# Attention outputs kept as features by tokens, their softmax sums turned by DMA, and GpSimd and SyncE in program order

## The chip, the cores and the metric

One core of a Trainium2 chip runs the whole program. Its engines are TensorE (PE; PEld is its weight load), VectorE (DVE), ScalarE (ACT), GpSimd (POOL) and SyncE (SP, which only issues transfers). The metric is the device time of one execution in microseconds.

## The reference

A block with adaptive layer norm, softmax attention and a gated feed-forward part, all in float32:

```python
# x: 2048 tokens x 576; 32 heads of 18; the feed-forward width is 4608
x = A_x
mod = (silu(c) @ w_mod)                          # sa, ca, ga, sb, cb, gb: 576 each
h = layernorm(x) * (1 + ca) + sa
q, k, v = (h @ wqkv) split into 32 heads of 18
p = softmax(q @ k.T * 18 ** -0.5)
o = p @ v                                        # heads side by side: 2048 x 576
x = x + ga * (o @ wo)
h = layernorm(x) * (1 + cb) + sb
x = x + gb * ((sigmoid(h @ w_gate) * (h @ w_up)) @ w_down)
```

## The kernel before

There are three stages. The first normalizes the tokens and projects q, k and v. The second is attention, with much other work laid into it. The third ("gated" stage) computes the feed-forward part, with two levels of sums and differences of blocks that save products.

**Attention.** The loop over `u` has 32 units: a half of the tokens (1024 queries) times a pair of heads. Inside, `kt` runs over 16 tiles of 128 keys. Work is written out for pairs of steps by the strings in `STEPS`: `t` is a score product of a head and a chunk of 512 queries, followed by its exponential on ACT; `m` is one of the 64 products per unit whose row maxima DVE takes for a coming unit (`maxima`, driven by `turn`, 24 products ahead); `V`, or `A` and `B` in halves, is the product of exponentials and values (`values`) for all four head-chunks at once. The values have a column of ones, so that the 19th of each 32 result rows is the softmax sum. The result of a unit is a bank of 128 partitions (4 groups of 32: head, chunk) by 512 queries: features by tokens.

When a unit is done, `taken` copies the bank to `oT` on ACT (L673). `outputs`, in the pair at `kt` 2 of the next unit, turns it with four transposes on PE (L683), copies it back to `oT` on ACT (L699), takes reciprocals on DVE (L702) and multiplies on GpSimd (L705) into a table of tokens by features: `Oa` for the first half, a tile `big` for the second, together the list `Os`. For `kt` 2 and 4 there are orders of their own in `STEPS`.

Other work goes along one piece per pair, at the letter `G`. `down_parts` (units 4 to 14, on GpSimd) splits and scales `w_down`; `first_rows` (step 240 to 439) projects tiles 0 to 7 of the first half's rows with `wo` and prepares the operands of the gated stage; `last_rows_project` (from step 440) projects tiles 8 to 15, from 384 of the 576 features. Both use `project_o`, which transposes each tile of the table back to features by tokens on PE (L772, L789), copies it by DVE (L778) and splits it into a high and a low part on GpSimd (L779, L780). Where a coming piece has products, the pair is "heavy" and takes the order `full`, with whole value products; else the pair is "halved". A heavy pair at `kt` 2 or 12 is put off (`hold`).

`spread` turns the maxima of a unit into two rows of its queries (four small transfers, L590). `load_heads(u + 2)` loads queries and keys of the unit after the next by eight transfers on SyncE, at the start of unit `u`. The queries' and keys' buffers are those of unit `u - 1`.

The remaining 192 features of the second half are stored (`oend`) and projected in `last_rows`, a generator that runs between the products of the gated stage and transposes them again (L1526, L1534).

**What sets the order.** Engines named in `manual_schedule` keep the order in which the program emits their instructions. The others get an order from the framework's planner, by its own costs. In attention PE and ACT were named; SyncE, DVE and GpSimd were planned. From the eighth product of the gated stage on, PE, DVE and ACT are named. Every engine executes its queue in order, so an instruction that waits holds those behind it. `paced` makes an instruction wait for the last exponential emitted so far.

Of the kernel before, what the change touches and what calls it, by code (L numbers as in the profile page):

```python
# [23 lines left out]
P = 128  # L24
S = 2048
# [62 lines left out]
def tile_block(ctx, tc, x_in, wqkv, wo, w_gate, w_up, w_down, c_in, w_mod, out):  # L88
# [206 lines left out]
    oend = dram.tile([P, 8, D - DL], F32, name="oend")  # L295
# [338 lines left out]
    Os = [Oa]  # L634
# [33 lines left out]
    def taken():  # L668

        if "whole" in state:  # L670
            half, p, acc = state.pop("whole")
            oT = epool.tile([P, 512], F32, name="oT")
            nc.scalar.copy(oT, acc)  # L673
            state["end"] = (half, p, oT)

    def outputs():

        if "end" not in state:
            return
        half, p, oT = state.pop("end")  # L680
        tp = bank().rearrange("p (b q) -> p b q", q=P)
        for b in range(4):
            nc.tensor.transpose(tp[:, b, :], oT[:, b * P : (b + 1) * P], ident)  # L683

        yield
        tq = tp.rearrange("p b (j e) -> p j b e", e=32)
        rec = epool.tile([P, 4, 4], F32, name="rec")
        if half == 1 and p == H // 2 - 1:
            nc.vector.reciprocal(rec, tq[:, :, :, DH])
            state["last"] = epool.tile([P, 512], F32, name="oT")[:, 0 : 16 * DH].rearrange("p (t e) -> p t e", t=8)  # L690
            for h in range(2):
                nc.vector.tensor_tensor(
                    state["last"][:, :, h * DH : (h + 1) * DH].rearrange("p (c b) e -> p c b e", c=2),
                    tq[:, 2 * h : 2 * h + 2, :, 0:DH],
                    rec[:, 2 * h : 2 * h + 2, :].unsqueeze(3).to_broadcast([P, 2, 4, DH]),
                    op=ALU.mult,
                )
            return
        nc.scalar.copy(oT, tp.rearrange("p b q -> p (b q)"))  # L699
        yield  # L700
        tq = oT.rearrange("p (b j e) -> p j b e", j=4, e=32)
        nc.vector.reciprocal(rec, tq[:, :, :, DH])  # L702
        for h in range(2):
            f0 = (2 * p + h) * DH
            nc.gpsimd.tensor_tensor(  # L705
                Os[half][:, :, f0 : f0 + DH].rearrange("p (c b) e -> p c b e", c=2),
                tq[:, 2 * h : 2 * h + 2, :, 0:DH],
                rec[:, 2 * h : 2 * h + 2, :].unsqueeze(3).to_broadcast([P, 2, 4, DH]),
                op=ALU.mult,
            )  # L710


# [4 lines left out]
    def load_wo():  # L717
# [31 lines left out]
        for _ in range(4):  # L749
            yield  # L750
# [3 lines left out]
    def project_o(t):  # L754

        wo_h, wo_l, we = weights
        if t <= 8:
            held_rows[:] = temp([P, 2048], F32R), temp([P, 2048], F32)
        T, T_ = held_rows
        if t < 8:  # L760
            xt, full, od = T_[:, 0:D], T_[:, 1024:1536], T_[:, 1536:1664]
        else:
            T, T_ = T[:, 1024 * (t % 2) : 1024 * (t % 2) + 1024], T_[:, 960 * (t % 2) : 960 * (t % 2) + 960]
            xt, full = T_[:, 0:D], T_[:, D : D + 384]
        nc.gpsimd.dma_start(xt, x_rows[:, t, :])
        src = Os[t // 8][:, t % 8, :]
        n = 4 if t < 8 else DL // P
        oh = T[:, 0 : n * P]
        ol = T[:, 512 : 512 + n * P]
        pt = bank()  # L770
        for i in range(n):
            nc.tensor.transpose(pt[:, i * P : (i + 1) * P], src[:, i * P : (i + 1) * P], ident)  # L772
        if t >= 12:
            nc.vector.tensor_copy(oh, pt[:, 0 : n * P])
            nc.vector.tensor_sub(ol, pt[:, 0 : n * P], oh.bitcast(F32))  # L775
        else:
            full = full[:, 0 : n * P]
            nc.vector.tensor_copy(full, pt[:, 0 : n * P])  # L778
            nc.gpsimd.tensor_copy(oh, full)  # L779
            nc.gpsimd.tensor_sub(ol, full, oh.bitcast(F32))  # L780
        yield None if t < 8 else "g"
        if t < 8:
            om = T[:, 1024:1152]
            omh = T[:, 1152:1280]
            nc.gpsimd.tensor_copy(
                od.rearrange("p (a e) -> p a e", e=64), src[:, DM:D].unsqueeze(1).to_broadcast([P, 2, 64])
            )
            pt = bank()
            nc.tensor.transpose(pt[:, 0:P], od, ident)  # L789
            nc.vector.tensor_copy(od, pt[:, 0:P])  # L790
            nc.gpsimd.tensor_copy(om[0:64], od[0:64])
            nc.gpsimd.tensor_copy(omh[64:P], od[64:P])
            nc.gpsimd.tensor_sub(om[64:P], od[64:P], omh[64:P].bitcast(F32))
            yield "g"
        for h in range(2):
            cols = slice(h * HALF, (h + 1) * HALF)
            ts_ = []
            for i in range(n):
                a, b = oh[:, i * P : (i + 1) * P], ol[:, i * P : (i + 1) * P]
                ts_ += [(a, wo_h[:, i, cols]), (a, wo_l[:, i, cols]), (b, wo_h[:, i, cols])]  # L800
            if t < 8:
                ts_ += [(om, we[:, 0, cols]), (om, we[:, 1, cols])]
            acc = bank()
            for i, (a, w) in enumerate(ts_):
                nc.tensor.matmul(acc[:, :HALF], a, w, start=i == 0, stop=i == len(ts_) - 1)  # L805
            to = Oa[:, t, :] if t < 8 else xt
            nc.vector.tensor_add(to[:, cols], xt[:, cols], acc[:, 0:HALF])
            yield None if h else "g"
        if t >= 8:
            nc.gpsimd.dma_start(x1p[:, t - 8, :], xt)  # L810
# [64 lines left out]
    def first_rows():  # L875
        yield from load_wo()
        for t in range(8):
            yield from project_o(t)
# [118 lines left out]
    def last_rows_project():  # L997
        for t in range(8, NT):
            yield from project_o(t)

# [36 lines left out]
    rows1 = last_rows_project()  # L1037
    downs = down_parts()
    for u in range(UNITS):
        half, p = divmod(u, H // 2)  # L1040
        qs, ks = heads(u)
        if 0 < u < UNITS - 2:
            load_heads(u + 2)
        if u == H // 2:
            Os.append(big.tile([P, 8, 640], F32, name="big"))
        for kt in range(NT):
# [3 lines left out]
            if kt % 2 == 0:  # L1050
                heavy = state.get("next") == "g"
                hold = heavy and (kt == 2 or kt == 12 and u < UNITS - 1)
                halved = step >= 10 and (hold or not heavy)
                rows = FROM0 <= step < FROM1
                order = two_steps(STEPS["full" if not halved else "rows" if rows else kt if kt in STEPS else "half"])
            probs = [None] * 4
            for does, h, c in order[kt % 2]:
# [4 lines left out]
                elif does in "OSG":  # L1062
                    if halved and kt == 2:
                        follow.append(outputs())
                        next(follow[-1], None)
# [23 lines left out]
            pending.append((half, p, kt, probs))  # L1089
            if u in (1, 3):  # L1090
# [29 lines left out]
            if u == UNITS - 1 and kt == 3:  # L1120
                nc.sync.dma_start(oend[:, :, 0 : D - DL - 2 * DH], Os[1][:, :, DL : D - 2 * DH])
# [12 lines left out]
    for _ in outputs():  # L1134
        pass
    manual.close()
    nc.sync.dma_start(oend[:, :, D - DL - 2 * DH :], state["last"])
# [373 lines left out]
    def last_rows():  # L1511

        def psum():
            return pd.tile([P, 512], F32, name="d")

        with tc.tile_pool(name="fin", bufs=1, side="right") as pool:
            w = pool.tile([P, 2, 2, D], F32R, name="w")
            nc.gpsimd.dma_start(w, wod)
            for t0 in (0, 4):
                od = pool.tile([P, 4, 256], F32, name="od")  # L1520
                nc.sync.dma_start(od[:, :, 0:192], oend[:, t0 : t0 + 4, :])
                nc.sync.dma_start(od[:, :, 192:256], oend[:, t0 : t0 + 4, 128:192])
                yield 1.4, 5 if t0 == 0 else 2
                pt = psum()
                for j in range(4):
                    nc.tensor.transpose(pt[:, j * P : (j + 1) * P], od[:, j, 0:P], ident)  # L1526
                oh = pool.tile([P, 512], F32R, name="oh")
                ol = pool.tile([P, 512], F32R, name="ol")
                nc.vector.tensor_copy(oh, pt)
                nc.vector.tensor_sub(ol, pt, oh.bitcast(F32))  # L1530
                yield 1.4, 1
                pt = psum()
                for j in range(4):
                    nc.tensor.transpose(pt[:, j * P : (j + 1) * P], od[:, j, P:256], ident)  # L1534
                om = pool.tile([P, 512], F32R, name="om")
                omh = pool.tile([P, 512], F32R, name="omh")
                nc.vector.tensor_copy(om[0:64], pt[0:64])
                nc.vector.tensor_copy(omh[64:P], pt[64:P])
                yield 0.7, 0
# [278 lines left out]
```

## Time and profile before

| | |
|---|---|
| median of 3 runs | 2801.53 us (2798.26 to 2804.0) |
| profiled execution: time, span | 2804.88 us, 2803.1 us |
| granted TensorE clock, mean | 0.998 |
| busy PE, DVE, ACT, POOL | 2771.9, 2306.3, 1609.3, 814.6 us |
| attention | first exponential at 236.1 us, last value products until 1532.9 us |

The profiled execution took 2804.88 us, of which the span, first to last instruction, is 2803.1. In the profile's rows a time in front is a start in microseconds from the span's begin, then the duration, the engine, the line of the kernel, the operation and `out<-in` by the program's names, with the number of instructions merged in the row. In rows of groups, busy time and the mean duration in nanoseconds follow the bar, then the idle time of the engine ahead of them and what ended it. Buffers from `bank` are called `s`, those of the rows' temporaries `t`.

### The profile page before, as it was taken

What the parts mean: (1) busy time and instruction counts of PE and PEld (TensorE: products, weight loads), DVE (VectorE), ACT (ScalarE), POOL (GpSimd) and SP (SyncE); (2) the same over time, 40 slices, a digit from 0 to 9 for tenths busy, and PEclk for the clock granted to TensorE, in tenths of its full rate; (3) what the DMA queues carried; (4) which work ended last, traced back from release to release, by engine and by line L of the source; (5) the groups of instructions that cost most, each with busy time, mean ns of one, the idle gap of its engine ahead of it and who ended that gap; (6) DMA issues with size and microseconds to landing.
All of it is one profiled execution on the core that took longest, in us unless ns stands there. A gap on an engine that the chain in (4) does not pass through costs nothing.

```text
span 2803.1 us, 50644 instructions
## 1 busy us (share of the span) xinstructions
PE 2771.9 (99%) x18637; PEld 1847.4 (66%) x18637; DVE 2306.3 (82%) x4370; ACT 1609.3 (57%) x3051; POOL 814.6 (29%) x1077
## 2 busy tenths in 40 slices
PE   7999999999999999999999999999999999999999
PEld 5975444444444444444444888888888888888888
DVE  7278999999998888999883778888898677777777
ACT  3215999999999878999888332333333222222221
POOL 3125207888843111663103222232221100000000
PEclk9999999999999999999999999999999999999999
DMA  5344224444432120232127766667767956566653
GB/s 172 121 157 140 78 61 162 171 169 166 172 133 82 36 58 24 98 106 71 43 68 227 273 222 223 240 213 273 278 245 280 339 195 201 194 200 195 200 195 120
DMA packets 170777, 462.59 MB, mean 165 GB/s; under 512 B 21212, under 2 KB 88032, under 8 KB 160416
## 3 DMA queue, kind: packets, MB, share of 16 engines
q1 hardware_dynamic: 150064, 360.72, 38.4%
q0 software_dynamic: 20464, 98.62, 9.9%
q8 instruction: 147, 2.41, 0.4%
q14 instruction: 102, 0.84, 0.1%
HBM read 281.92 MB, written 176.82 MB: 164 GB/s over the span
## 4 chain that ended last, share of the span: by engine, by line
PE 92%; DVE 4%; DMA 2%; issue 2%; POOL 0%; ACT 0%; SPq 0%; DVEq 0%; ACTq 0%; POOLq 0%
PE x L1225 26%; PE o L656 19%; PE s L1084 12%; PE s L550 11%; PE d L1375 8%; PE d L1307 6%; PE s L336 4%; PE s L805 2%; PE s L389 1%; DMA out_dram<-Oa 1%; DVE mx L556 1%; PE s L683 1%; DMA wq_raw<-in_A_wqkv_dram 1%; DVE w L1215 0%; DVE Oa L1379 0%
## 5 line engine op out<-in xcount | busy, mean ns | idle before, releaser
L1088 ACT ACTIVATE p<-s 128x512 f32<-128x512 f32 x2048 | 1069.1, 616 | 89.2 <-PE s L1084 62.6
L556 DVE TENSOR_REDUCE mx<-s 128x1 f32<-128x512 f32 x1568 | 1000.9, 683 | 101.3 <-PE s L550 75.1
L656 PE MATMUL o<-p,vaug 128*32 128x256 f32 (+1 forms) x5848 | 595.1, 478 | 0.1
L550 PE MATMUL s<-k,q 54*128 54x512 f32 x1920 | 548.6, 434 | 2.0 <-DVE t L775 1.0
L1084 PE MATMUL s<-q,k 56*128 56x512 f32 x1920 | 527.7, 440 | 0.0
L550 PEld LDWEIGHTS s<-k,q 54*128 54x128 f32 x1920 | 273.4, 184 | 231.9 <-DVE mx L561 88.0
L1084 PEld LDWEIGHTS s<-q,k 56*128 56x128 f32 x1920 | 249.8, 184 | 232.1 <-ACT p L1088 72.9
L1225 PE MATMUL x<-k,w 128*128 128x512 f32 x1512 | 370.0, 392 | 0.0
L1225 PEld LDWEIGHTS x<-k,w 128*128 128x128 f32 x1512 | 276.8, 188 | 53.3 <-PE o L656 0.8
L1375 PE MATMUL d<-wd,hh 128*128 128x288 f32 x1248 | 249.9, 295 | 2.4 <-DVE Oa L1379 2.4
L656 PEld LDWEIGHTS o<-p,vaug 128*32 128x32 f32 x5848 | 116.2, 108 | 203.1 <-issue 187.5
L1225 PE MATMUL x<-big,w 128*128 128x512 f32 x1008 | 245.5, 392 | 0.7 <-DVE u L1724 0.7
L1225 PE MATMUL x<-w,w 128*128 128x512 f32 x1008 | 245.3, 391 | 0.0
L1225 PEld LDWEIGHTS x<-big,w 128*128 128x128 f32 x1008 | 185.1, 188 | 37.0 <-DVE u L1724 1.1
L1225 PEld LDWEIGHTS x<-w,w 128*128 128x128 f32 x1008 | 184.3, 188 | 34.5
L1375 PEld LDWEIGHTS d<-wd,hh 128*128 128x128 f32 x1248 | 202.2, 188 | 6.2 <-DVE Oa L1379 3.1
L1375 PE MATMUL d<-wd,hl 128*128 128x288 f32 x624 | 184.3, 295 | 0.0
L1379 DVE TENSOR_TENSOR Oa<-Oa,d 128x288 f32<-128x288 f32 x312 | 136.6, 453 | 55.1 <-PE d L1375 51.2
L561 DVE CUSTOM_DVE_ANT_0 over<-s,over 128x512 f32<-128x512 f32 x240 | 163.9, 683 | 1.3 <-PE s L1084 1.2
L559 ACT ACTIVATE over<-s 128x512 f32<-128x512 f32 x240 | 145.8, 608 | 11.3 <-PE s L550 9.3
L1234 ACT ACTIVATE sg<-x 128x512 f32<-128x512 f32 x36 | 21.6, 599 | 210.2 <-PE x L1225 210.2
L1206 ACT CAST w<-S 128x768 fp32r<-128x768 f32 x71 | 59.4, 836 | 137.8 <-POOL S L1179 136.0
(275 smaller groups left out, 3898.5 us busy)
## 6 DMA issues: line engine op xcount, KB each, us to landing
ws<-w SPq DMA_DIRECT2D x126, 640.0 KB
w<-ws SPq DMA_DIRECT2D x126, 640.0 KB
wd<-wds SPq DMA_DIRECT2D x19, 1152.0 KB
k<-kd SPq DMA_DIRECT2D x60, 360.0 KB
wds<-w POOLq DMA_DIRECT2D x18, 1152.0 KB, 5.2
wtd<-t POOLq DMA_DIRECT2D x32, 576.0 KB, 5.0
wt<-wtd SPq DMA_DIRECT2D x64, 288.0 KB
wd<-wds SPq DMA_DIRECT2D x52, 288.0 KB
```

Source lines behind the costliest of these rows:

```text
L336: nc.tensor.matmul(acc, w, hT[:, t, cols], start=n == 0, stop=n == len(ts_) - 1)
L550: nc.tensor.matmul(sp, qs[rows, qt * P : (qt + 1) * P], ks[rows, at * 512 : (at + 1) * 512], start=True, stop=True,)
L556: nc.vector.tensor_reduce(to, sp, axis=AX.X, op=ALU.max)
L559: nc.scalar.activation(over, sp, AF.Relu)
L561: nc.vector.tensor_tensor_reduce(out=over, in0=sp, in1=over, scale=1.0, scalar=LOWEST, op0=ALU.add, op1=ALU.max, accum_out=mx[:, h * n + q ...
L656: nc.tensor.matmul(acc[32 * j : 32 * j + 32, cols], vaug[:, kt, (2 * p + h) * VW : (2 * p + h) * VW + 32], probs[2 * c + h][:, cols], star ...
L1084: nc.tensor.matmul(sT, ks[rows, kcols], qs[rows, c * 512 : (c + 1) * 512], start=True, stop=True)
L1088: state["exp"] = nc.scalar.activation(pr, sT, AF.Exp, scale=SCALE)
L1225: nc.tensor.matmul(acc[v], w[:, v, a, :], X[s][:, b, :], start=first and n == 0, stop=n == 6, skip_group_check=not first,)
L1307: nc.tensor.matmul(acc, a[:, rows], w[:, k, :], start=n == 0, stop=n == 2)
L1375: nc.tensor.matmul(acc[:, :HALF], a[:, f, rows], w[:, f, cols], start=n == 0, stop=n == 5)
L1379: nc.vector.tensor_add(Oa[:, t, cols], Oa[:, t, cols], acc[:, :HALF])
```

## The change

The outputs stay features by tokens, so nothing is transposed on PE on their account.

- `taken` copies the bank to `oT`, then stores the four rows of sums (4 x 512) to memory and loads them as 128 x 16 (`sT`). The new `outputs`, a generator advanced at the letter `c`, takes their reciprocals on DVE at `kt` 2 (paced), stores them, loads them repeated over 32 partitions each (`R`, 128 x 512), multiplies `oT` by `R` on GpSimd at `kt` 6 (paced), and at `kt` 14 stores the four blocks of 18 features to `ot` in memory.
- `load_rows` loads rows of `ot` (features by tokens) into `big`, 128 features at a time, at units 14 and 16 for the first half, 26 and 27 for the second.
- `project_rows` replaces `project_o`: `rows_parts` splits a tile's columns of `big` on GpSimd alone, one tile ahead; the products and additions are as they were. Two segments per tile remain of four or three; a pause of ten instead of four pieces follows `load_wo`.
- The orders for `kt` 2 and 4 go, and with them the holding of heavy pairs at `kt` 2.
- `load_heads(u + 2)` moves from the start of the unit to behind `kt` 4.
- SyncE and GpSimd are named in attention's `manual_schedule`.
- The last unit's sums and outputs go through `lastd`; `last_rows` loads the sums, takes reciprocals and multiplies on DVE, without transposes.

```diff
-    2: "V m1t0 t1t0 m0m1 O A c m1r0 t1m0 t1t0 G B c x0t1 m1t0",
-    4: "V r0m1 t1t0 m1m0 G A c t0t1 m1t0 B t1m0 m1t0 t1x0",
...
     def taken():
...
+        sT = epool.tile([P, 16], F32, name="sT")
+        to = osums[half * H // 2 + p, 0]
+        nc.sync.dma_start(to, oT[DH::32, :])
+        nc.sync.dma_start(sT, to.rearrange("j (q r) -> (j q) r", r=16))
+        follow.append(outputs(half, p, oT, sT))
+
+    def outputs(half, p, oT, sT):
+
+        while state["kt"] < 2:
+            yield
+        rec = epool.tile([P, 16], F32, name="rec")
+        paced(nc.vector.reciprocal(rec, sT))
+        to = osums[half * H // 2 + p, 1]
+        nc.sync.dma_start(to.rearrange("j (q r) -> (j q) r", r=16), rec)
+        R = state["room"] if "room" in state else bgp.tile([P, 512], F32, name="R")
+        nc.sync.dma_start(R, to.unsqueeze(1).to_broadcast([4, 32, 512]))
         yield
-        for b in range(4):
-            nc.tensor.transpose(tp[:, b, :], oT[:, b * P : (b + 1) * P], ident)
...
+        while state["kt"] < 6:
+            yield
+        paced(nc.gpsimd.tensor_mul(R, oT, R))
         yield
+        while state["kt"] < (8 if state["u"] == UNITS - 1 else 14):
+            yield
         for h in range(2):
+            for c in range(2):
+                f0, n0, j = (2 * p + h) * DH, half * HW + c * 512, 2 * h + c
+                nc.sync.dma_start(ot[f0 : f0 + DH, n0 : n0 + 512], R[32 * j : 32 * j + DH, :])
...
+    def rows_parts(t):
...
+        nc.gpsimd.dma_start(xt, x_rows[:, t, :])
+        src = state["rows"][:, 0:n, cols]
...
+        nc.gpsimd.tensor_copy(oh3, src)
+        nc.gpsimd.tensor_sub(ol3, src, oh3.bitcast(F32))
...
+    def project_rows(t0):
+
+        if t0:
+            for _ in range(5):
+                yield
+        ahead = rows_parts(t0)
+        yield
+        yield "g"
...
+                if h == 0 and t < t0 + 7:
+                    ahead = rows_parts(t + 1)
+                if h == 1 and t >= 8:
+                    nc.gpsimd.dma_start(x1p[:, t - 8, :], xt)
+                yield "g" if t < t0 + 7 or h == 0 else None
...
-    manual.enter_context(tc.manual_schedule(engines={mybir.EngineType.PE, mybir.EngineType.Activation}))
+    manual.enter_context(
+        tc.manual_schedule(engines={mybir.EngineType.PE, mybir.EngineType.Activation, mybir.EngineType.SP, mybir.EngineType.Pool})
+    )
...
-        if 0 < u < UNITS - 2:
-            load_heads(u + 2)
...
-                hold = heavy and (kt == 2 or kt == 12 and u < UNITS - 1)
+                hold = heavy and kt == 12 and u < UNITS - 1
...
             pending.append((half, p, kt, probs))
+            if kt == 4 and 0 < u < UNITS - 2:
+                load_heads(u + 2)
...
+            for j in range(4):
+                one = lastd[32 * j + DH : 32 * j + DH + 1, :]
+                nc.sync.dma_start(sT[32 * j : 32 * j + 32, :], one.rearrange("l (q r) -> l q r", r=16))
+            yield 0.1, 2
+            nc.vector.reciprocal(sT, sT)
...
+                nc.sync.dma_start(od[:, 0, :], ot[DL:DM, n0 : n0 + 512])
...
+                nc.gpsimd.memset(R, 1.0)
+                for p0 in (0, 64):
+                    p1 = p0 + 64 - 2 * DH
+                    nc.sync.dma_start(end[p0:p1], ot[DM : D - 2 * DH, n0 : n0 + 512])
+                    for h in range(2):
+                        j, p2 = 2 * h + c, p1 + h * DH
+                        nc.sync.dma_start(end[p2 : p2 + DH], lastd[32 * j : 32 * j + DH, :])
+                        nc.sync.dma_start(R[p2 : p2 + DH], to[j : j + 1, :].to_broadcast([DH, 512]))
...
+                nc.vector.tensor_mul(end, end, R)
```

More of the change, by code (lines that the diff above doesn't have):

```diff
@@ L294, in tile_block @@
     x1p = dram.tile([P, 8, D], F32, name="x1p")
-    oend = dram.tile([P, 8, D - DL], F32, name="oend")
+    ot = dram.tile([D, S], F32, name="ot")
+    osums = dram.tile([UNITS, 2, 4, 512], F32, name="osums")
+    lastd = dram.tile([P, 512], F32, name="lastd")
     wod = dram.tile([P, 2, 2, D], F32R, name="wod")
@@ L668, in taken @@
     def taken():
[L670 to L678, printed above, removed]
-            return
-        half, p, oT = state.pop("end")
-        tp = bank().rearrange("p (b q) -> p b q", q=P)
-        for b in range(4):
-            nc.tensor.transpose(tp[:, b, :], oT[:, b * P : (b + 1) * P], ident)
-        yield
[L686 to L699, printed above, removed]
@@ new lines, in taken @@
+        if "whole" not in state:
+            return
+        half, p, acc = state.pop("whole")
+        oT = epool.tile([P, 512], F32, name="oT")
+        nc.scalar.copy(oT, acc)
+        if half == 1 and p == H // 2 - 1:
+            nc.sync.dma_start(lastd, oT)
+            return
+        sT = epool.tile([P, 16], F32, name="sT")
[3 more added lines that the diff above has]
+        follow.append(outputs(half, p, oT, sT))
@@ L748, in load_wo @@
         weights.extend((wo_h, wo_l, we))
-        for _ in range(4):
+        for _ in range(10):
             yield
     held_rows = []
-    def project_o(t):
-        wo_h, wo_l, we = weights
[L757 to L810, printed above, removed]
@@ new lines, in load_rows @@
+    def load_rows(half, tiles):
+        own = slice(half * HW, (half + 1) * HW)
+        for i in tiles:
+            if i < 4:
+                nc.sync.dma_start(state["rows"][:, i, :], ot[i * P : (i + 1) * P, own])
+            else:
+                for p0 in (0, 64):
+                    nc.sync.dma_start(state["rows"][p0 : p0 + 64, 4, :], ot[DM:D, own])
+    def rows_parts(t):
+        if t % 8 == 0:
+            held_rows[:] = temp([P, 2048], F32R), temp([P, 2048], F32)
+        T, T_ = (a[:, 1024 * (t % 2) : 1024 * (t % 2 + 1)] for a in held_rows)
+        n = 4 if t < 8 else DL // P
+        cols = slice(t % 8 * P, (t % 8 + 1) * P)
+        xt = T_[:, 0:D]
+        nc.gpsimd.dma_start(xt, x_rows[:, t, :])
+        src = state["rows"][:, 0:n, cols]
+        oh, ol = (T[:, a : a + n * P] for a in (0, 512))
+        oh3, ol3 = (a.rearrange("p (i q) -> p i q", q=P) for a in (oh, ol))
+        nc.gpsimd.tensor_copy(oh3, src)
+        nc.gpsimd.tensor_sub(ol3, src, oh3.bitcast(F32))
+        om = None
+        if t < 8:
+            om, omh = bgp.tile([P, P], F32R, name="om", bufs=2), T_[:, 640:768].bitcast(F32R)
+            end = state["rows"][:, 4, cols]
+            nc.gpsimd.tensor_copy(om[0:64], end[0:64])
+            nc.gpsimd.tensor_copy(omh[64:P], end[64:P])
+            nc.gpsimd.tensor_sub(om[64:P], end[64:P], omh[64:P].bitcast(F32))
+        return n, oh, ol, om, xt
@@ new lines, in project_rows @@
+    def project_rows(t0):
[5 more added lines that the diff above has]
+        yield "g"
+        wo_h, wo_l, we = weights
+        for t in range(t0, t0 + 8):
+            n, oh, ol, om, xt = ahead
+            for h in range(2):
+                cols = slice(h * HALF, (h + 1) * HALF)
+                ts_ = []
+                for i in range(n):
+                    a, b = oh[:, i * P : (i + 1) * P], ol[:, i * P : (i + 1) * P]
+                    ts_ += [(a, wo_h[:, i, cols]), (a, wo_l[:, i, cols]), (b, wo_h[:, i, cols])]
+                if t < 8:
+                    ts_ += [(om, we[:, 0, cols]), (om, we[:, 1, cols])]
+                acc = bank()
+                for i, (a, w) in enumerate(ts_):
+                    nc.tensor.matmul(acc[:, :HALF], a, w, start=i == 0, stop=i == len(ts_) - 1)
+                to = Oa[:, t, :] if t < 8 else xt
+                nc.vector.tensor_add(to[:, cols], xt[:, cols], acc[:, 0:HALF])
+                if h == 0 and t < t0 + 7:
[3 more added lines that the diff above has]
+                yield "g" if t < t0 + 7 or h == 0 else None
@@ L876, in first_rows @@
         yield from load_wo()
-        for t in range(8):
-            yield from project_o(t)
+        yield from project_rows(0)
         for t in range(8):
@@ L1041, in tile_block @@
         qs, ks = heads(u)
-        if 0 < u < UNITS - 2:
-            load_heads(u + 2)
-        if u == H // 2:
-            Os.append(big.tile([P, 8, 640], F32, name="big"))
+        if u in (14, 26):
+            state["big"] = big.tile([P, 8, 640], F32, name="big").rearrange("p a b -> p (a b)")
+            state["rows"] = state["big"].rearrange("p (i n) -> p i n", n=HW)
+            if u == 26:
+                state["room"] = state["big"][:, 4 * HW : 4 * HW + 512]
+            load_rows(u // 26, range(3) if u == 14 else range(2))
         for kt in range(NT):
@@ L1061, in tile_block @@
                     taken()
[L1062 to L1065, printed above, removed]
+                elif does in "SG":
                     if "spread" in state:
@@ L1119, in tile_block @@
                 load_x(u - 30, f"k{u - 30}")
-            if u == UNITS - 1 and kt == 3:
-                nc.sync.dma_start(oend[:, :, 0 : D - DL - 2 * DH], Os[1][:, :, DL : D - 2 * DH])
+            if (u, kt) == (16, 1):
+                load_rows(0, (3,))
+            if (u, kt) == (16, 15):
+                load_rows(0, (4,))
+            if (u, kt) == (27, 15):
+                load_rows(1, (2,))
             if u == UNITS - 1 and kt == 9:
@@ L1518, in last_rows @@
             nc.gpsimd.dma_start(w, wod)
-            for t0 in (0, 4):
[L1520 to L1526, printed above, removed]
+            sT = pool.tile([P, 16], F32, name="sT")
@@ new lines, in last_rows @@
+            for j in range(4):
[3 more added lines that the diff above has]
+            nc.vector.reciprocal(sT, sT)
+            to = osums[UNITS - 1, 1]
+            nc.sync.dma_start(to.rearrange("j (q r) -> (j q) r", r=16), sT)
+            for t0 in (0, 4):
+                c = t0 // 4
+                n0 = HW + 512 * c
+                od = pool.tile([P, 2, 512], F32, name="od")
+                nc.sync.dma_start(od[:, 0, :], ot[DL:DM, n0 : n0 + 512])
+                end = od[:, 1, :]
+                omh = pool.tile([P, 512], F32R, name="omh")
+                R = omh.bitcast(F32)
+                nc.gpsimd.memset(R, 1.0)
+                for p0 in (0, 64):
+                    p1 = p0 + 64 - 2 * DH
+                    nc.sync.dma_start(end[p0:p1], ot[DM : D - 2 * DH, n0 : n0 + 512])
+                    for h in range(2):
+                        j, p2 = 2 * h + c, p1 + h * DH
+                        nc.sync.dma_start(end[p2 : p2 + DH], lastd[32 * j : 32 * j + DH, :])
+                        nc.sync.dma_start(R[p2 : p2 + DH], to[j : j + 1, :].to_broadcast([DH, 512]))
+                yield 1.1, 3 if t0 == 0 else 2
@@ L1527, in last_rows @@
                 oh = pool.tile([P, 512], F32R, name="oh")
                 ol = pool.tile([P, 512], F32R, name="ol")
-                nc.vector.tensor_copy(oh, pt)
-                nc.vector.tensor_sub(ol, pt, oh.bitcast(F32))
+                nc.vector.tensor_copy(oh, od[:, 0, :])
+                nc.vector.tensor_sub(ol, od[:, 0, :], oh.bitcast(F32))
                 yield 1.4, 1
-                pt = psum()
-                for j in range(4):
-                    nc.tensor.transpose(pt[:, j * P : (j + 1) * P], od[:, j, P:256], ident)
@@ L1535, in last_rows @@
                 om = pool.tile([P, 512], F32R, name="om")
[L1536 to L1538 removed]
+                nc.vector.tensor_mul(end, end, R)
+                nc.vector.tensor_copy(om[0:64], end[0:64])
+                nc.vector.tensor_copy(omh[64:P], end[64:P])
                 yield 0.7, 0
[L1540 removed]
+                nc.vector.tensor_sub(om[64:P], end[64:P], omh[64:P].bitcast(F32))
```

20 lines of the change are left out of this document (2 added, 18 removed).

## The prediction

> **What bounds the kernel now.** I read the page's engine table and its chain first, then the windows by stage, then one unit of attention in the timeline of every engine.
>
> ```profile
> PE 2771.9 (99%) x18637; PEld 1847.4 (66%) x18637; DVE 2306.3 (82%) x4370; ACT 1609.3 (57%) x3051; POOL 814.6 (29%) x1077
> PE 92%; DVE 4%; DMA 2%; issue 2%; POOL 0%; ACT 0%; SPq 0%; DVEq 0%; ACTq 0%; POOLq 0%
> 600.00:700.00 100.00, 100.00 (x851) 43.10 (x851) 93.55 (x177) 97.79 (x197) 81.50 (x131) 1.00 0.47 167
> 1000.00:1100.00 100.00, 98.81 (x770) 46.31 (x767) 86.38 (x179) 83.02 (x165) 20.69 (x34) 1.00 0.15 43
> 1536.00:1700.00 164.00, 162.58 (x909) 143.82 (x908) 129.16 (x228) 50.18 (x76) 40.54 (x37) 1.00 0.70 242
> ```
>
> TensorE never rests: 99% busy, 92% of the chain that ended last, at a granted clock of 1.00. But the windows (columns: PE, PEld, DVE, ACT, POOL busy, clock, DMA share, GB/s) show two kinds of attention. In 600–700 us ("light" units, no row work) ACT is at 97.8% and DVE at 93.6% too; in 1000–1100 us (rows projected) both fall to 83–86% and PE alone sets the pace. So a microsecond taken from PE is a microsecond gained in the row units and the gated stage, while in light units ACT must lose as much. It does: look at unit 10.
>
> ```profile
> 624.93 1.07 PE L656 MATMUL o<-p,vaug 128*32 128x512 f32 x8
> 629.73 1.06 PE L656 MATMUL o<-p,vaug 128*32 128x512 f32 x8
> 631.62 0.66 PE L683 MATMUL s<-ident,oT 128*128 128x128 f32 x4
> 632.21 0.64 PE L656 MATMUL o<-p,vaug 128*32 128x256 f32 x8
> 635.06 1.07 PE L656 MATMUL o<-p,vaug 128*32 128x512 f32 x8
> 639.67 1.06 PE L656 MATMUL o<-p,vaug 128*32 128x512 f32 x8
> 648.98 1.07 PE L656 MATMUL o<-p,vaug 128*32 128x512 f32 x8
> 653.64 1.06 PE L656 MATMUL o<-p,vaug 128*32 128x512 f32 x8
> 663.21 1.07 PE L656 MATMUL o<-p,vaug 128*32 128x512 f32 x8
> 628.90 0.63 ACT L673 COPY oT<-o 128x512 f32<-128x512 f32 x1
> 632.80 0.65 ACT L699 COPY oT<-s 128x512 f32<-128x512 f32 x1
> 633.55 0.25 DVE L702 RECIPROCAL rec<-oT 128x16 f32<-128x16 f32 x1 [0.40 <-ACT oT L699]
> ```
>
> Each whole value product opens a pair of steps. A unit of eight pairs takes 663.21 - 624.93 = 38.28 us. The four pairs from 635.06 to 653.64 take 4.65 us each; the pair at kt 2, with the four output transposes, takes 635.06 - 629.73 = 5.33. That pair costs 0.68 us more: 0.59 is the transposes (631.62 to 632.21), the rest a stall beside the second ACT copy.
>
> **The change part by part.**
>
> *Output transposes.* Gone: four transposes a unit and ACT's second copy. I take 0.68 us a unit; the ends are 0.59 (transposes alone) and 0.72 (against the fastest pair, 639.67 - 635.06 = 4.61). Units 1 to 31 give 31 x 0.68 = 21.1 us. ACT loses its 0.65 copy at the same place, so its floor moves with PE's. DVE stays at 0.936 x 38.28 = 35.8 us a unit, under the 37.6 that remain. The last unit's transposes sit ahead of the next stage's products: another 0.5.
>
> *Transposes of the rows.*
>
> ```profile
> 281.00:1536.00 1255.00, 9.63 (x56) 5.83 (x56) 1.00 0.32 106
> 281.00:1536.00 1255.00, 2.52 (x8) 1.11 (x8) 1.00 0.32 106
> 1536.00:1700.00 164.00, 1.20 (x8) 0.99 (x8) 1.00 0.70 242
> L778 DVE COPY t<-s 128x512 f32<-128x512 f32 x8 | 5.5, 682 | 0.0
> L780 POOL TENSOR_TENSOR t<-t,t 128x512 fp32r<-128x512 f32 x8 | 10.3, 1283 | 0.4
> L705 POOL TENSOR_TENSOR Oa<-oT,rec 128x144 f32<-128x144 f32 x32 | 13.1, 431 | 97.8 <-DVE rec L702 97.6
> ```
>
> The first three are the windows of L772, L789 and L1526 alone (L1534 has the same row as L1526). The 64 transposes in attention are 12.15 us busy. Each record's modelled end overlaps the next instruction; at 0.59/4 = 0.15 apiece they are 9.6. I take 10.5. The gated stage's sixteen are 2 x 1.20 = 2.4. PE is the bound in both places, so all counts. The 16 + 16 product segments remain 37 whole-value pairs in both versions, by their order of emission; the changed one packs them closer, and unit 31, without maxima, keeps none. DVE's copies (8 x 0.68 and smaller ones) go too; DVE has idle time there, so nothing more.
>
> *GpSimd.* Two multiplies of 0.43 us become one 128x512 tensor-tensor, 1.28 us by the L780 row: +0.42 a unit. At 81.5% busy it has 7 us idle a unit; a row tile's copy and split (under 2 x 1.28 us, and pieces of 64 partitions) stand beside two pairs' products. Nothing, unless its program order blocks it: the multiply waits for the broadcast R, and behind it queue the `w_down` splits and GpSimd's own DMA issues. What those write is read after attention, and the multiply's own readers, the stores, come eight steps later, so a wait of 3 us for R is covered by the same 7 us.
>
> *The sums' chain and SyncE's queue.* New per unit, in SyncE's program order: sums out (waits for the copy), sums in (waits for landing), reciprocal on DVE, out again, broadcast R (waits for landing), then at kt 4 the eight loads of `load_heads`, at kt 12 the four of `spread`, at kt 14 four stores. No row of the small round trip exists; the nearest are the gates' two-row write and the read that waits for it, twice, and the loads of unit 10:
>
> ```profile
> 325.06 0.51 SPq L198 DMA_DIRECT2D gates<-w  x2
> 330.54 0.35 SPq L199 DMA_DIRECT2D ga_b<-gates  x1
> 403.32 0.52 SPq L198 DMA_DIRECT2D gates<-w  x2
> 406.31 0.36 SPq L199 DMA_DIRECT2D gb_b<-gates  x1
> 624.59 0.79 SPq L514 DMA_DIRECT2D q<-qd  x1
> 629.96 0.48 SPq L522 DMA_DIRECT2D k<-kd  x1
> 649.97 0.49 PE L550 MATMUL s<-k,q 54*128 54x512 f32 x1
> ```
>
> The second of two writes is issued 0.26 us after the first, so write to landing is 406.31 - 403.58 = 2.7 us undisturbed, 330.54 - 325.32 = 5.2 with a large load behind it. In unit 10's clock: copy done 629.53, sums back after two legs at 634.9, reciprocal 635.3, reciprocals landed 638.0, R issued, loads issued over the 5.85 us that 624.59 to 630.44 shows, so until 644.2, landed 646.9 to 649.4. They are needed when the maxima of unit u+2 begin, by the counter `turns` in the pair at kt 10, at 649.97. Cover 0.6 to 3.1 us: thin, but I book nothing. The four `spread` transfers and four stores come later and have a pair each. The bytes added (R 256 KB, outputs 144 KB a unit, ten row loads) meet a DMA share of 0.47.
>
> The Trainium skill, "DMA: Bandwidth & Descriptors", section "Anatomy of one DMA", puts about 2.0 us on any transfer, mostly the write's receipt; these rows say 2.7, the trace decides, and by 2.0 the chain would only be 2 us shorter and the sum the same.
>
> *The reciprocal's wait.* DVE alone keeps the planner's order. The reciprocal is paced by an exponential at kt 2 (about 632), its sums arrive at 634.9. If the planner queues it at the pace, DVE stands 2.9 us a unit with the maxima behind it, and PE waits for their banks; if it queues it on arrival, nothing. Ends: 0, and 2.9 less about 1.2 us (four banks of scores at 4.65/16 = 0.29) = 1.7 in the 27 units whose kt 2 pair is halved. Nearest row: L702 above, queued 0.40 us early on a wait that a planner also had to guess. With half of that reaching PE: 0.2 x 27 = 5.4 us lost.
>
> *Gated stage.* DVE gains a reciprocal and two multiplies of about 0.7 us, with 35 us idle in 1536–1700. SyncE gains some 26 issues at about 0.4 us and two round trips, with the raw weights' loads behind. 0 to 5 us; I take 1, PE's idle time there being 1.4 in all.
>
> **Sum.** 21.1 + 0.5 + 10.5 + 2.4 = 34.5 gained, 5.4 + 1 = 6.4 lost: 28.1 faster. The profiled execution took 2804.88 us (span 2803.1); less 28.1 is 2776.8. The median of the runs is 3.35 lower, so 2773.
>
> The Trainium skill, "TensorE: Matmul & The Clock Gate", section "Part 4: PE-mode transpose", gives about 275 ns per transpose in a kernel; 208 would then be an estimated 57 us, and the time 2751. The trace has 272-ns records, but they overlap: four in 0.59 us.
>
> **Rivals.**
> *The loads come late (slower).* Place: SyncE's queue, eight loads behind the sums' chain. If each of three legs takes 5.2 instead of 2.7 us, loads land 7.5 later, 4.4 to 6.9 past need, and PE stands at kt 10. For: the DMA engines are half busy with `w_down` blocks in units 4 to 14. Against: 2.7 us in the quiet case, and bursts fill only part of a unit. Price 11 x 4.4 = 48: 2821. It decides from 28.1/4.4, some seven such units.
>
> *The reciprocal holds DVE.* At the full 1.7 us in 27 units 46 are lost: 2804.9 - 3.35 - 34.5 + 46 + 1 = 2814. It eats the gain from 1.24 us a unit. For: L702 shows it queued early; against: early by 0.4 only, and DVE has 2.5 us idle a unit.
>
> *Light units keep their time*, because ACT or DVE, not PE, sets it. For: 97.8% and 93.6%. Then the rows and gated terms remain, 10.5 + 2.4 + 0.5 less 1 = 12.4: 2789. Against: ACT loses the copy too.
>
> *Transposes dearer than their spacing* (0.275 each on the path, were the 272-ns records not overlapped): 2751.
>
> **How the numbers follow.** Forecast 0.60 (2760 to 2786). Light units unchanged or half the gain lost to DVE 0.15 (2786 to 2795). Reciprocal's wait near 1.2 us, no change, 0.09. Loads late 0.09 and the reciprocal at its full price 0.05, slower; dearer transposes 0.02, faster. With 0.2% (5.6 us, about what a measurement tells): faster 0.75, same 0.10, slower 0.15. Range 2760 to 2803: down to the stall-free 2767 and a margin, up to where the no-change cases begin; 2 in 10 lie outside.
>
> **What would show it.** No matmul on `oT`, `big` or `od` with `ident`; light pairs all near 4.65 us and a unit at 37.6; units 18, 19, 29 with seven or five whole-value pairs in a row; ACT with one copy a unit. Wrong, if idle time of DVE before the reciprocal exceeds 1 us each with the sums' DMA as its releaser, if PE's weight loads at kt 10 wait for a `k` or `q` transfer, or if light units stay at 38.3.

## The result, and the profile after

The changed kernel takes 2917.99 us (median of 4 runs), the kernel before 2799.9: a ratio of 1.0427, with an interval of 1.0403 to 1.0451. It is slower by 118 us, where 28 us faster was forecast. The profiled execution's span is 2915.6 us against 2803.1.

The page of the changed kernel, its engine table and chain:

```profile
PE 2803.7 (96%) x18429; PEld 1847.8 (63%) x18429; DVE 2293.3 (79%) x4342; ACT 1597.8 (55%) x3020; POOL 840.6 (29%) x1048
PE 78%; DMA 13%; DVE 3%; issue 2%; SPq 1%; ACT 1%; POOL 1%; DVEq 0%; ACTq 0%; POOLq 0%
```

TensorE has 208 matmuls fewer and is busy 32 us longer, and transfers, 2% of the chain before, are 13%. TensorE's own waits name one of them (total, times, longest):

```profile
PE s L550 <- DMA k<-kd: 75.4, 20, 8.1
```

L550 is the product whose maxima DVE takes; it waits for the keys of the unit after the next, the loads that the change moved. The kernel before has no wait for `k` in its list. The exponentials' row gives the extent of attention, before and after (first and last start): 1295.1 us became 1409.5. What follows the last exponential is 1271.9 us of the span before and 1271.4 after, so the whole loss lies in attention.

```profile
L1088 ACT ACTIVATE p<-s x2048: 570/604/765, 236.1 to 1531.2; 128x512 f32<-128x512 f32 x187
```

```profile
L1081 ACT ACTIVATE p<-s x2048: 569/607/782, 234.7 to 1644.2; 128x512 f32<-128x512 f32 x187
```

Unit 10 of the changed kernel in the timeline of SyncE, ACT and TensorE:

```profile
682.91 0.64 ACT L673 COPY oT<-o 128x512 f32<-128x512 f32 x1
683.57 0.55 SPq L679 DMA_DIRECT2D osums<-oT  x1
685.31 0.35 SPq L680 DMA_DIRECT2D sT<-osums  x1
687.96 0.34 SPq L690 DMA_DIRECT2D osums<-rec  x1
689.44 0.58 SPq L692 DMA_DIRECT2D R<-osums  x1
690.08 0.79 SPq L514 DMA_DIRECT2D q<-qd  x1
695.27 0.49 SPq L522 DMA_DIRECT2D k<-kd  x1
693.11 1.06 PE L655 MATMUL o<-p,vaug 128*32 128x512 f32 x8
697.74 1.06 PE L655 MATMUL o<-p,vaug 128*32 128x512 f32 x8
702.37 1.06 PE L655 MATMUL o<-p,vaug 128*32 128x512 f32 x8
708.39 0.54 PE L550 MATMUL s<-k,q 54*128 54x512 f32 x1 [4.53 <-DMA k<-kd]
714.47 1.54 PE L655 MATMUL o<-p,vaug 128*32 128x512 f32 x8
```

The pair at kt 8 takes 702.37 - 697.74 = 4.63 us, the pair at kt 10 takes 714.47 - 702.37 = 12.10. Of the 7.5 us too many, 4.53 are the wait. The rest is in the windows of the same stretch (columns as in the prediction: the column before the DMA share is the granted clock):

```profile
702.00:704.00 2.00, 1.87 (x13) 0.42 (x11) 1.96 (x5) 1.91 (x5) 2.00 (x3) 1.00 0.82 336
704.00:706.00 2.00, 0.00 (x0) 0.00 (x0) 0.17 (x1) 0.50 (x1) 1.79 (x3) 1.00 0.67 242
706.00:708.00 2.00, 0.00 (x0) 0.00 (x0) 0.00 (x0) 0.00 (x0) 0.02 (x1) 1.00 0.94 310
708.00:710.00 2.00, 1.60 (x9) 0.91 (x13) 0.86 (x2) 0.97 (x2) 1.50 (x2) 0.66 0.39 154
710.00:712.00 2.00, 2.00 (x16) 0.62 (x12) 1.52 (x3) 0.55 (x2) 1.92 (x4) 0.50 0.00 0
712.00:714.00 2.00, 2.00 (x14) 0.91 (x14) 0.57 (x2) 1.32 (x4) 1.84 (x4) 0.50 0.00 0
714.00:716.00 2.00, 2.00 (x14) 0.26 (x10) 1.62 (x4) 1.39 (x3) 1.84 (x5) 0.63 0.00 0
```

After the stall the granted clock is 0.66, 0.50, 0.50 and 0.63 in four windows of 2 us. That loses 3.4 us of full clock, or 6.8 us at half clock, in which TensorE is "busy" but slow. Stretches like this one are where the added busy time comes from (32 us net, though 208 matmuls are gone): the mean granted clock is 0.973 here and was 0.998.

### The profile page after: what moved, and what is told of

Same layout as the page of the kernel before. It is cut to its first block, busy times and chain, and to the rows that moved or that the text cites. A ratio compares the mean times of both kernels' runs of the same rounds, so it can differ in the third digit from the quotient of the medians.

```text
span 2915.6 us, 50784 instructions
## 1 busy us (share of the span) xinstructions
PE 2803.7 (96%) x18429; PEld 1847.8 (63%) x18429; DVE 2293.3 (79%) x4342; ACT 1597.8 (55%) x3020; POOL 840.6 (29%) x1048
## 4 chain that ended last, share of the span: by engine, by line
PE 78%; DMA 13%; DVE 3%; issue 2%; SPq 1%; ACT 1%; POOL 1%; DVEq 0%; ACTq 0%; POOLq 0%
PE x L1221 24%; PE o L655 15%; PE s L1077 10%; PE s L550 9%; DMA k<-kd 7%; PE d L1371 7%; PE d L1303 6%; PE s L336 3%; PE s L799 2%; DMA R<-osums 2%; PE s L389 1%; ACT p L1081 1%; DMA out_dram<-Oa 1%; DMA osums<-rec 1%; DVE mx L556 1%
## 5 line engine op out<-in xcount | busy, mean ns | idle before, releaser
L550 PE MATMUL s<-k,q 54*128 54x512 f32 x1920 | 575.8, 452 | 79.5 <-DMA k<-kd 75.4
L655 PE MATMUL o<-p,vaug 128*32 128x256 f32 (+1 forms) x5848 | 618.5, 494 | 0.2 <-ACT oT L673 0.2
L1077 PE MATMUL s<-q,k 56*128 56x512 f32 x1920 | 558.2, 455 | 2.7 <-DVE mx L556 2.4
L550 PEld LDWEIGHTS s<-k,q 54*128 54x128 f32 x1920 | 290.2, 193 | 305.9 <-issue 86.5
L1077 PEld LDWEIGHTS s<-q,k 56*128 56x128 f32 x1920 | 263.1, 192 | 263.0 <-DVE mx L556 80.8
```

The costliest lines, as they stand in the source:

```text
L550: nc.tensor.matmul(sp, qs[rows, qt * P : (qt + 1) * P], ks[rows, at * 512 : (at + 1) * 512], start=True, stop=True,)
L655: nc.tensor.matmul(acc[32 * j : 32 * j + 32, cols], vaug[:, kt, (2 * p + h) * VW : (2 * p + h) * VW + 32], probs[2 * c + h][:, cols], star ...
L1077: nc.tensor.matmul(sT, ks[rows, kcols], qs[rows, c * 512 : (c + 1) * 512], start=True, stop=True)
```

## The experiments

Theory L: the loads are late, TensorE stands at kt 10 and is slow after it. Rival G: GpSimd's program order puts its stores where they collide. Rival S: the new small transfers and stores cost by themselves.

**Loads back at the unit's start.**

```diff
+        if 0 < u < UNITS - 2:
+            load_heads(u + 2)
         if u in (14, 26):
...
-            if kt == 4 and 0 < u < UNITS - 2:
-                load_heads(u + 2)
```

> The changed kernel with load_heads(u + 2) back at the start of unit u, ahead of the sums' transfers in SyncE's order; everything else stays. Theory L (the eight loads go out 9 us into the unit behind the sums' chain, land after kt 10 beside GpSimd's own transfers, TensorE stands and its clock falls): TensorE's 75.4 us of waits for k nearly vanish, the granted clock in attention is back at 1.00, and the time is 2765 to 2800; the sums now queue behind eight loads, so the reciprocal may wait some 3 us a unit. Rival G (GpSimd's program order puts its stores where they collide, wherever the loads stand): still above 2860. Rival S (small transfers of sums and stores slow everything): above 2850.

2831.37 us, ratio 1.0112 (1.0095 to 1.0129). TensorE's wait for `k` is gone from its list, and 87 us of the 118 with it; but the time is above the range given, and the mean granted clock is 0.986. What stands there now:

```profile
PE s L167 <- POOL big L141: 21.3, 4, 10.2
PE s L910 <- POOL z L890: 7.8, 4, 6.8
```

L167 is the modulation's product in units 2 and 4, L910 a transpose of the first half's rows, both behind GpSimd. Its timeline, and SyncE's, in unit 1:

```profile
283.14 0.57 SPq L679 DMA_DIRECT2D osums<-oT  x1
298.04 0.35 SPq L680 DMA_DIRECT2D sT<-osums  x1
307.37 0.59 SPq L692 DMA_DIRECT2D R<-osums  x1
293.50 0.74 POOL L138 TENSOR_SCALAR big<-big,sc 128x576 f32<-128x576 f32 x1 [39.68 <-DMA big<-in_w_mod_dram]
312.57 1.29 POOL L696 TENSOR_TENSOR R<-oT,R 128x512 f32<-128x512 f32 x1 [18.33 <-DMA R<-osums]
313.84 1.46 POOL L138 TENSOR_SCALAR big<-big,sc 128x576 f32<-128x576 f32 x2
```

The store of 8 KB of sums goes out behind the keys' and the modulation's loads on the same queue, and the read that waits for its landing goes out 14.9 us later. So R is late, GpSimd stands 18.33 us at the multiply, and the scaling of the modulation's weights, next in its program order, starts at 313.84, too late for the product in unit 2. This is a second cost of the change, and it shows only when the first is removed.

**GpSimd left to the planner.**

```diff
-... mybir.EngineType.SP, mybir.EngineType.Pool})
+... mybir.EngineType.SP})
```

> The changed kernel with GpSimd left to the planner in attention, SyncE still in program order; loads stay behind kt 4. Theory L: GpSimd's stores move a little in the unit, the loads still come at 9 us and late; 2870 to 2940. Rival G: the collision goes, 2765 to 2800.

2909.78 us, inside theory L's range, ratio 1.0402 (1.0374 to 1.043), with `PE s L550 <- DMA k<-kd` at 73.3 us in 20 waits. GpSimd's order is not the cause; rival G falls.

**The kernel before, loads made late.** In `load_heads` each transfer is wrapped in `paced`, and the call stands behind kt 3:

```diff
-        if 0 < u < UNITS - 2:
-            load_heads(u + 2)
...
             pending.append((half, p, kt, probs))
+            if kt == 3 and 0 < u < UNITS - 2:
+                load_heads(u + 2, paced)
```

> The kernel before with one thing changed: the eight loads of load_heads(u + 2) each wait for the last exponential of kt 3, so that they go out some 9.5 us into unit u, as in the changed kernel, without its sums' chain, its stores or its orders. Theory L: TensorE waits for k at kt 10, the clock falls in those units, 2880 to 2980. Rivals G and S: lateness alone is covered, 2795 to 2825.

2834.33 us, ratio 1.0124 (1.0109 to 1.0139): far less than theory L gave, and more than the rivals did. And with kt 5 in place of kt 3:

> The kernel before with the loads of load_heads(u + 2) waiting for the last exponential of kt 5 instead of kt 3, so that they go out about 11.9 us into the unit (9.4 in the run before this one; 8.9 to 17 in the changed kernel). Theory L: in quiet units they landed at +20.8 to +21.5 us, with need at about +23, so 2.4 us more takes nearly every unit over the edge: TensorE waits for k in some 25 units, half-clock stretches follow, 2870 to 2960. Rival (the loads' place costs about 35 us however late they are, the rest is the sums' and stores' traffic): 2830 to 2850.

2996.72 us, ratio 1.071 (1.0694 to 1.0726), above the range given. TensorE's waits in the two, kt 3 first:

```profile
PE s L550 <- DMA k<-kd: 14.7, 8, 4.1
```

```profile
PE s L550 <- DMA k<-kd: 106.0, 27, 8.7
```

Times within a unit are counted from its first exponential, and a unit's length from there to the next unit's. The loads went out at 9.4 us in a light unit with kt 3, and at 14.2 with kt 5 (11.9 had been expected: the exponentials of kt 5 end later than I had counted). One place costs 35 us, one 4.8 us further down 198. It is an edge, as theory L has it: at 9.4 us only units with GpSimd's own transfers beside the loads miss it; the changed kernel's loads go out between 8.9 us and 17.0, and 20 of 29 units miss it. So lateness alone can cost more than the change did. But the place is not the whole of it. Twelve units of the changed kernel sent their first load before 10 us, and 8 of them waited, 22.3 us in all; 22 units did so in the kernel with kt 3, and 7 waited, 13.1 us in all. What slows the loads further in the changed kernel is not shown; R's 256 KB go out just ahead of them on the same queue there.

**Program order alone in the kernel before.**

```diff
-... engines={mybir.EngineType.PE, mybir.EngineType.Activation}
+... engines={mybir.EngineType.PE, mybir.EngineType.Activation, mybir.EngineType.SP, mybir.EngineType.Pool}
```

> The kernel before with SyncE and GpSimd named in attention's program order, nothing else. Theory L: loads still go out at the unit's start, so within 0.5% of before, 2786 to 2815. Rival G: the order alone costs 50 us or more.

2812.57 us, ratio 1.0048 (1.0033 to 1.0063): inside the range, a small loss. In the profiled execution, 7.5 us longer by its span, all of it is in unit 30 (50.7 us against 42.5), where TensorE's longest wait in attention ended on DVE's addition of row results (5.9 us). What delayed that was not followed up.

**The change without the sums' transfers.**

```diff
-        nc.sync.dma_start(to, oT[DH::32, :])
-        nc.sync.dma_start(sT, to.rearrange("j (q r) -> (j q) r", r=16))
+        nc.gpsimd.memset(sT, 1.0)
...
-        nc.sync.dma_start(to.rearrange("j (q r) -> (j q) r", r=16), rec)
-        nc.sync.dma_start(R, to.unsqueeze(1).to_broadcast([4, 32, 512]))
+        nc.gpsimd.memset(R, 1.0)
```

> The changed kernel, loads still behind kt 4 in the program, without the four transfers of the sums: sT and R are set to one by GpSimd, so the outputs are not divided by their sums. The reciprocal, the multiply, the four stores, the rows and all orders stay. Theory L: nothing in front of the loads waits, SyncE reaches them at the unit's start, TensorE does not wait for k, 2760 to 2795. Rival (stores of outputs, rows and program order cost by themselves): above 2830.

2773.48 us, ratio 0.9907 (0.9894 to 0.9921). `load_heads` is still called behind kt 4, but nothing ahead of it in SyncE's queue waits, so the loads go out at the unit's start. Stores, rows, multiplies and orders stay, so the part of rival S that blames the stores falls: the chain in front of the loads is what made them late, and the rest of the change gains 25 us. This kernel leaves out the division by the sums, and with it the sums' transfers, so whether these cost by themselves is left to the kernels below, which keep all of them.

**Mended: loads first, sums later.** On top of the first experiment:

```diff
-        while state["kt"] < 2:
+        last = state["u"] == UNITS - 1
+        while state["kt"] < (2 if last else 8):
...
-        while state["kt"] < 6:
+        while state["kt"] < (6 if last else 12):
...
             if u in (1, 3):
-                if kt == 0:
+                if kt == 2:
```

> The changed kernel with load_heads at the unit's start, the reciprocal at kt 8 and the multiply at kt 12 (2 and 6 before; the last unit as it was), and the modulation's loads of units 1 and 3 emitted behind kt 2, after the sums' write and read, instead of kt 0. Theory L with its second part (small transfers queue behind the bulk of SyncE's loads, and GpSimd, in program order, stands at the multiply with TensorE's next operands behind it): the pairs of 20 to 30 us in units 2, 4 and 22 go, TensorE does not wait for k, 2755 to 2785, faster than both. If the second part is wrong, about 2830 as with the loads first alone.

2778.88 us, ratio 0.993 (0.9918 to 0.9943): 0.7% faster than the kernel before, with every transfer of the sums in place, so the rest of rival S falls too. Its page:

```profile
PE 2740.3 (99%) x18429; PEld 1828.6 (66%) x18429; DVE 2288.3 (82%) x4342; ACT 1590.9 (57%) x3020; POOL 842.2 (30%) x1048
```

Its timeline, with the value products that open the pairs of unit 11 from kt 0:

```profile
653.00 1.07 PE L655 MATMUL o<-p,vaug 128*32 128x512 f32 x8
657.78 1.07 PE L655 MATMUL o<-p,vaug 128*32 128x512 f32 x8
662.50 1.06 PE L655 MATMUL o<-p,vaug 128*32 128x512 f32 x8
667.16 1.07 PE L655 MATMUL o<-p,vaug 128*32 128x512 f32 x8
```

TensorE is busy 31.6 us less than before, and the pair at kt 2 takes 4.72 us where it took 5.33.

**The same, GpSimd planned.**

> The same with GpSimd left to the planner. Theory L: with the multiply late enough to wait for nothing, program order and planner come within 0.5% of each other, 2750 to 2795. Rival (GpSimd's program order costs by itself): over 15 us faster than the same kernel in program order.

2800.87 us, ratio 1.0017 (0.9996 to 1.0038): the planner costs 22 us here by the medians (ten runs from 2792.6 to 2819.2, against 2776.9 to 2783.0), so theory L's half per cent was wrong, and the rival's sign too. ACT's and GpSimd's rows in unit 16 say how a part of it comes about:

```profile
854.09 0.59 ACT L673 COPY oT<-o 128x512 f32<-128x512 f32 x1 [6.75 <-POOL R L697]
847.02 1.41 POOL L730 TENSOR_TENSOR t<-t,ga_b 128x576 f32<-128x576 f32 x1 [3.07 <-DMA t<-in_A_wo_dram]
852.78 1.27 POOL L697 TENSOR_TENSOR R<-oT,R 128x512 f32<-128x512 f32 x1
```

The planner put the preparation of `wo` ahead of the multiply; the multiply frees `oT`, the next copy waits for it, and ACT and TensorE with it. That makes unit 16 45.9 us long, against 37.9 in program order, out of 17.5 us between the spans of the two profiled executions. Unit 30 is 6.5 us longer too, where TensorE waits 7.4 us for the rows of maxima (`q<-mrows`); why was not followed up. In program order the multiply has its turn. So naming GpSimd in the schedule is worth its place once the loads are right.

**The change with the sums later, and nothing else.** The two limits of the mended kernel (kt 8 and 12), with `load_heads` behind kt 4:

> The changed kernel with the reciprocal at kt 8 and the multiply at kt 12 alone; load_heads stays behind kt 4, which now puts it ahead of the reciprocals' store and the broadcast in SyncE's order, with only the landing of the sums' write in front. Theory L: loads go out some 5 to 7 us into the unit, 16 to 18 us ahead of need, TensorE hardly waits for k except in units 1 and 3, where the modulation's weights stand in front: 2780 to 2810, as against 2918 for the change as made. Rival (any place behind the sums' write is too late): above 2850.

2780.27 us, ratio 0.9934 (0.9918 to 0.9951), with no wait for `k` in TensorE's list. SyncE in unit 10:

```profile
620.63 0.55 SPq L679 DMA_DIRECT2D osums<-oT  x1
622.93 0.35 SPq L680 DMA_DIRECT2D sT<-osums  x1
623.38 0.82 SPq L514 DMA_DIRECT2D q<-qd  x1
628.36 0.48 SPq L522 DMA_DIRECT2D k<-kd  x1
638.41 0.36 SPq L691 DMA_DIRECT2D osums<-rec  x1
```

Now the loads stand behind one landing, not three, and go out 2.8 us after the sums' store, where unit 10 of the changed kernel took 6.5. Two numbers are the difference between 2918 and 2780 us, and what the mended kernel does beyond them shows no gain (ratios 0.993 and 0.9934).

## Why the prediction was wrong

**The step that failed** is "The sums' chain and SyncE's queue": the landing of the eight loads. The step found the place, the queue, the need at kt 10 and a thin cover of 0.6 to 3.1 us, and booked nothing. Counted from the end of the copy, it had the loads go out from about 9 us to 14.7, landed by 17.4 to 19.9, needed at 20.4. In unit 10 (copy done at 683.55) they went out from 6.5 to 12.2, earlier than that, and `k` came at 24.8. The mis-sized term is the landing: 2.7 to 5.2 us after the last issue were taken from transfers of a few KB, for a burst that is 1.5 MB by the sizes in the profile's list of issues. From the last issue to the product that waited it took 708.39 - 695.76 = 12.6 us, with the transfer engines at 0.67 to 0.94 of their time in the windows above, up to the wait's end, GpSimd's transfers among them. Over the 20 units that waited, the first load went out 10.5 us into the unit in the median (9.1 to 13.8; the copy ends at 2.5), about as forecast, and from the last issue to the product it took 10.3 (8.0 to 12.7). With kt 5 in the kernel before it took 7.5.

The profile of the kernel before had this figure. In its unit 27, SyncE's last load goes out at 1326.24, for 0.49 us, and GpSimd's queue moves nothing beside it:

```profile
1326.24 0.49 SPq L522 DMA_DIRECT2D k<-kd  x1
1328.00:1330.00 2.00, 2.00 (x20) 0.90 (x18) 1.78 (x3) 2.00 (x5) 0.00 (x0) 1.00 0.57 160
1330.00:1332.00 2.00, 2.00 (x20) 0.80 (x22) 1.67 (x4) 1.97 (x5) 0.82 (x2) 1.00 0.60 184
1332.00:1334.00 2.00, 2.00 (x22) 0.65 (x14) 1.70 (x5) 2.00 (x5) 0.00 (x0) 1.00 0.07 20
```

The transfer engines work on the burst until after 1332, at least 5.3 us and at most 7.3 behind its last issue. Put behind 644.2, the end of issue in the prediction, that is 649.5 to 651.5, with need at 649.97: no cover worth the name, even without GpSimd's transfers. The prediction's own sign of being wrong, a wait of TensorE at kt 10 for `k`, came true in 20 units.

**The rival that came true** was priced at 2821 with a chance of 0.09. It counted only units 4 to 14 and only the wait. For these units its 48 us are close to the 45.2 measured, which is luck: it had the legs of the chain late, and late was the landing. Outside them TensorE waited 30.2 us more, and half clock came on top. The balance of spans: TensorE's idle time rose from 31.2 us (2803.1 - 2771.9) to 111.9, by 80.7. Its busy time is 63.4 above the mended kernel's 2740.3 for the same work; the records of the granted clock give 75 us lost to half clock in attention, a part of them while TensorE was idle, and 5 in the mended kernel. Less the 31.6 of work saved, that is 112.5, the difference of the spans. The half clock is absent from the forecast altogether. A cover of 0.6 us with a cliff behind it is not worth zero: the price of missing should have been multiplied by the chance of it, unit by unit. (The chances listed add up to 0.77 for faster and 0.14 for slower, where the forecast has 0.75 and 0.15; nothing hangs on that.)

**What held.** The gain of work was forecast as 34.5 us gross, and TensorE is busy 31.6 us less in the mended kernel. Of the 28.1 net, the kernel without the chain gains 24.8 and the mended one 19.4 by the medians (2798.3 - 2778.88). Output transposes: light units 37.6 to 37.7 us, against 38.3, as 0.68 a unit had it; the rival that light units keep their time falls. **What held in part:** the row units, 16 to 30, gained 12.1 us together in the mended kernel (639.7 to 627.6), where 0.68 a unit and the 10.5 of the rows' transposes make 20.7; where the rest went was not followed up. Program order on GpSimd, booked at nothing, cost nothing where R came early enough, and is then worth 22 us; with the loads first and the multiply at kt 6 it held GpSimd for 18.33 us. **What did not:** the gated stage's 2.4 us of transposes brought nothing (1272.0 us after the last exponential in the mended kernel, 1271.9 before): TensorE's waits for DVE after 1510 us rose from 5.2 to 8.4 us, more than the 1 us booked. And the reciprocal's wait, booked at 5.4 us, was hardly there: DVE's idle time before it is 12.4 us in 31 in the changed kernel, 6.0 in the mended one, and L702 had 15.8 before:

```profile
L688 DVE RECIPROCAL rec<-sT 128x16 f32<-128x16 f32 x31 | 7.6, 246 | 12.4 <-ACT p L1081 9.9 <-DMA sT<-osums 2.5
```

## What to carry to other kernels

In a queue that runs in program order, a waiting transfer delays every transfer behind it: put the bulk load with a deadline ahead of a chain of small dependent ones, or give the chain enough steps that its waits are over when its turn comes. Do not take the landing of a small transfer for that of a burst, and put the whole price of a miss against a thin cover. When an experiment removes one stall, look at what stands next before calling the rest small.

## What the runs showed of the hardware

A stall of TensorE cost more than its length: after 4.53 us of waiting the granted clock was 0.50 for 6.8 us, 3.4 us more lost. The Trainium skill, "TensorE: Matmul & The Clock Gate", section "What's actually happening", describes this: the clock is halved after at least one idle window of about 3.4 us and restored after at least one busy one. 6.8 us is two such windows, so the trace agrees with the window's length. It does not bear out that a wait must fill a window: 1.57 us in unit 11 of the changed kernel were followed by a granted clock of 0.76, 0.50 and 0.89 in the three windows of 2 us from 752, which is 3.4 us at half clock, while 2.78 us in unit 22 were followed by full clock.

A store of 8 KB let the read behind it wait for 14.9 us when about 4.1 MB of loads (eight of 1.5 MB together and the modulation's 2.6) had gone out before it on the same queue, and 7.7 us behind the eight loads alone (320.93 to 328.67 in the kernel with the loads first), against 1.7 us (683.57 to 685.31) where SyncE had sent nothing just before.

The eight loads of 1.5 MB took the transfer engines 5.3 to 7.3 us beyond their last issue when nothing ran beside them, and TensorE had `k` 8.0 to 12.7 us after the last issue in the units of the changed kernel that waited.
